# Scores of a head pair in one step over four PSUM banks, spatial mixing over 128 rows, and a new order of work

## The chip, the cores and the metric

The kernel runs on one core of one Trainium2 chip. The metric is device microseconds of one execution, lower is better; the median of three runs before the change is 319.94 us (319.62 to 322.25). Engines are named as in the profile: PE is TensorE's matmuls and PEld its weight loads, DVE is VectorE, ACT is ScalarE, POOL is GpSimd, SP is SyncE, whose queue issues the transfers.

## The reference

Three layers follow each other. All matrices are fp32, batch 2, sequence 448, model width 768.

```python
# 1: causal attention, 12 heads of 64
scores = where(causal, -1e9, q @ k.T / 8);  scores -= scores.max(-1)
a = exp(scores);  a = a / (a.sum(-1) + 1e-9);  x = a @ v
# 2: gated mixing along the sequence
h = gelu_tanh(x @ w_in);  u, v = h[..., :512], h[..., 512:]
v = (v - mean) / sqrt(var + 1e-6) * g_ln
v = einsum('ts,bsd->btd', w_sg, v) + b_sg          # the "spatial" mixing
x = x + (u * v) @ w_out
# 3: four attention experts, the best two of x @ w_gate by softmax weight
for e in range(4):
    out += weight[e] * (softmax(causal(q_e @ k_e.T / 8)) @ v_e @ wo[e])
```

## The kernel before

Everything stays on chip between the layers. Layer 1 works on pairs of heads: q and k of a pair are loaded (`qk_load`), rearranged into a `pair` tile by one copy, transposed on PE and copied to `qt` and `kt` with one head on rows 0 to 63 and the other on rows 64 to 127 (`qk_pair`). Scores of a pair are matmuls with 64 contraction rows, one head in each half of the PE array, side by side. The 448 query rows are four blocks (one of 64 rows and three of 128), causal, so that a head's scores fill two PSUM banks: bank 0 holds blocks 1 and 2 (192 and 320 keys), bank 1 holds block 3 (448 keys) and the 64-row block 0 (64 keys). `scores1(p, bank)` is one planner step for one bank of both heads. Then, for each head and bank, `bank_chain` runs: DVE adds the mask and takes the row maximum while it empties the bank (`tm`, L407), ACT takes the exponential and its sum (L414), DVE adds 1e-9 to the sums (L419) and takes reciprocals (L421), POOL or DVE scales `p` (L428, L430; in layer 3 with the gate, L426), PE transposes `p` (L434), and a copy brings it to `pt` (L359 on ACT, L361 on DVE). `pair_chain` multiplies by v (L460): 128 rows, 64 output columns a head, seven groups of matmuls for each head. Layer 3 does the same for two pairs of experts in each batch (`scores3`, L1148).

An fp32 matmul shows as two PE instructions (two passes); PE transposes and the float32r matmuls, which the projections use with high and low halves of each operand (three products each; L720, L681, L1181), show as one.

Layer 2 has the first projection in two parts: u in the transposed layout (`u_chain`, L720), v in the plain one (`v_chain`), both with a gelu. `sg_chain` transposes w_sg on PE (L825): four pieces of 112 rows and a fifth, a copy of the first 64 columns, because block 0 of both batches lies in one tile, batch 0 on rows 0 to 63 and batch 1 on rows 64 to 127. `spatial` (L909) is four fp32 matmuls in one PSUM bank: three over 128 rows and one over the 64 rows of block 0. Weights of w_in and w_out come as 64-bit words and are made into fp32 by ACT and DVE (`split64`, L504 to L510), then split into halves.

The order of all engines is set by a planner in the kernel (`Order`). Each piece of work is a generator that yields steps with a cost for each engine that may run them, buffers that they take (rings) and marks that they need. The planner keeps a clock for each engine and emits the step that can start first, within a slack by rank; ranks, biases for engines, buffer counts and the cost formulas are the numbers in `R`, `BIAS`, `SIZE` and the cost functions. What it emits is fixed at build time: on the chip each engine runs its list in order. The transfers are nearly all on SP's queue.

Of the kernel before, what the change touches and what calls it, by code (L numbers as in the profile page):

```python
# [58 lines left out]
def mm(n):  # L59
    return 2 + n / 2.4  # L60
# [18 lines left out]
class Step:  # L79
# [3 lines left out]
    def __init__(self, cost, take=(), need=(), dma=0, issue=450, kind=None, rows=1.0):  # L83
        self.cost, self.take, self.need, self.dma, self.issue = cost, take, need, dma, issue
        self.rows = rows
        self.bias = BIAS.get(kind, {})


def op(take=(), need=(), kind=None, rows=1.0, **cost):
    return Step(cost, take, need, kind=kind, rows=rows)  # L90
# [10 lines left out]
class Order:  # L101
# [12 lines left out]
    BIAS = dict(T=0, A=300, V=800, G=-400, S=0, Z=0)  # L114
    LATE = dict(T=0, A=300, V=700, G=-300, S=0, Z=0)
    TURN = 190000

    def __init__(self):
        self.clock = dict.fromkeys("TAVGSZ", 600.0)
        self.chains = []  # L120
        self.marks = {}
        self.rings = defaultdict(list)
        self.held = Counter()
        self.hw = self.queue = 0.0
        self.t, self.e = 0.0, "Z"
        self.used = defaultdict(float)
        self.state = (0, False)

    WINDOW = 10240 / 3

# [52 lines left out]
    def begin(self, ch):  # L185
# [13 lines left out]
        for e, c in st.cost.items():  # L199
# [9 lines left out]
            if e == "T" and not self.warm(t):  # L209
                c *= 2  # L210
# [6 lines left out]
    SLACK = 60  # L217

    def run(self):
        slack = self.SLACK  # L220
        while self.chains:
            first = {}
            cands = defaultdict(list)
            for ch in self.chains:
                b = self.begin(ch)
                if b is not None:
                    cands[b[0]].append((b[1], ch[0], ch, b[2], b[3]))
# [8 lines left out]
            e, (t, _, ch, items, end) = best  # L236
# [12 lines left out]
            else:  # L249
                self.t, self.e = end, e  # L250
                if e == "T":
                    self.use(t, end, st.rows)
                if e != "Z":
# [5 lines left out]
BIAS = {'ev': {'G': 100},  # L259
 'r': {'G': -600},  # L260
 'vh': {'A': -400, 'G': -200, 'V': 300},
 'vl': {'A': 400, 'V': 100},
 'wh': {'G': 400},
 'wl': {'A': 100},
 'y': {'G': 200, 'V': -200}}
R = dict(
    PV=(556.5, 563), PV0=556, vp=(569.5, 557.4), gt=(557.3, 543.0), QK=(555.5, 558.9, 562, 564),
    S=(552.4, 557, 560.3, 563), WO=(665.7, 669.3), WO0=669, v=(511, 517), v0=509, sp=(526, 538.7),
    wo2=(556.3, 546), wout=519, w3=(533, 555, 544.7), wo3=594, load=-37, trans=-7, vgroup=10, vhead=10, y=4,
    wu=4, wustep=4, wuahead=2, wv=58, wvafter=17, u=34, ub=(498.7, 481), sgl=63, sgafter=19, sgt=507,  # L270
    caps=(4, 2, 3, 5, 8, 7), av=0.5, bank=0.125, halves=28, bank3=1.125, av3=3.0, y3=14,
)
# [10 lines left out]
def attention_moe_kernel(  # L283
# [97 lines left out]
    class Core:  # L381


        def __init__(self, stack, side, n, np32, npt):
# [7 lines left out]
            ring("sm" + n, [ct([P, 4], F32, f"sm{n}{i}", pool) for i in range(4)])  # L392
            for _, _, t in o.rings["sm" + n]:
                G.memset(t, 1.0)
            ring("bias" + n, [ct([P, 4], F32, f"bias{n}{i}", pool) for i in range(6)])

    def bank_chain(c, key, bank, s, pts, pt_of, gate=None, need=()):
# [15 lines left out]
        for n, (i, rs, cs) in enumerate(parts):  # L413
            A.activation(p32[rs, cs], tm[rs, cs], AF.Exp, bias=bias[rs, i : i + 1], scale=-1.0,  # L414
                         accum_out=sm[rs, n : n + 1])
        give("tm" + c.n, tm)
        give("bias" + c.n, bias)
        yield op(V=73)
        V.tensor_scalar(sm[:, 0:2], sm[:, 0:2], 1e-9, None, op0=ALU.add)  # L419
        yield op(V=90)  # L420
        V.reciprocal(sm[:, 0:2], sm[:, 0:2])  # L421
        e, = yield op(kind="pr", G=950, V=500, need=need)
        for n, (i, rs, cs) in enumerate(parts):
            x, r = p32[rs, cs], sm[rs, n : n + 1]
# [19 lines left out]
    def pair_chain(c, b, keys, pts, vv, need, yh, yl, mark, after):  # L444


        _, y = yield op(T=2150, take=(BY,), need=[*[("p", k, bank) for k in keys for bank in range(2)], *need])
# [43 lines left out]
    def split64(src, shape, hi, lo, mark, rank=None):  # L491
# [4 lines left out]
        e, raw = yield dma(n * 2.84, ("raw",))  # L496
# [71 lines left out]
    def qk_load(p):  # L568
        b, hp = divmod(p, NP)
        raws = []  # L570
        for n, src in (("qraw", q), ("kraw", k)):
            e, t = yield dma(637, (n,), [("load", p - 1)] if p else ())
# [5 lines left out]
        done(("load", p))  # L578
# [38 lines left out]
    def qk_used(p):  # L617
        left["q", p] += 1
        if left["q", p] == 2:
            give("qt", qk[p][0])  # L620
            give("kt", qk[p][1])

    pts1 = defaultdict(dict)

    def scores1(p, bank):
# [12 lines left out]
        qk_used(p)  # L638
        for j, s in enumerate(ss):
            h = 2 * p + j  # L640
            o.add(2 * h + bank * R["bank"] * 8, bank_chain(core1, h, bank, s, pts1[h], lambda h=h: pt1_of(h)))
# [121 lines left out]
    for p in range(NPAIR):  # L763
        o.add(4 * p + R["load"], qk_load(p))
        for bank in range(2):
            o.add(4 * p + bank, scores1(p, bank))
# [16 lines left out]
    wsg, wvh, wvl = [], [], []  # L783
# [4 lines left out]
    def open_c2():  # L788
# [11 lines left out]
        for c in range(4):  # L800
            wsg.append(ct([P, SG], F32, f"wsg{c}", c2))
        u2[1] = [ct([P, S], F32, f"u2_1_{f}", c2) for f in range(4)]
# [486 lines left out]
```

## Time and profile before

| | before |
|---|---|
| timed runs, median (range) | 319.94 us (319.62 to 322.25) |
| profiled execution: span from first to last instruction | 317.5 us |
| busy in the span: PE | 302.2 us (95%) |
| DVE | 191.4 us (60%) |
| ACT | 173.7 us (55%) |
| POOL | 184.8 us (58%) |
| last chain: PE, POOL, DVE | 52%, 23%, 11% |

The profiled execution has no time of its own beside its span; the median of the timed runs is 2.44 us more than the span. PE instructions overlap in the records, so a share of 95% does not say that PE does useful work all the time. How closely matmuls follow each other is read from their start times.

Layer 1 lasts until the last L460 group, which starts at 125.34 us; the last `L1181` matmul is followed by one copy and the last transfer out.

### The profile page before, as it was taken

What the parts mean: (1) busy time and instruction counts of PE and PEld (TensorE: products, weight loads), DVE (VectorE), ACT (ScalarE), POOL (GpSimd) and SP (SyncE); (2) the same over time, 40 slices, a digit from 0 to 9 for tenths busy, and PEclk for the clock granted to TensorE, in tenths of its full rate; (3) what the DMA queues carried; (4) which work ended last, traced back from release to release, by engine and by line L of the source; (5) the groups of instructions that cost most, each with busy time, mean ns of one, the idle gap of its engine ahead of it and who ended that gap; (6) DMA issues with size and microseconds to landing.
All of it is one profiled execution on the core that took longest, in us unless ns stands there. A gap on an engine that the chain in (4) does not pass through costs nothing.

```text
span 317.5 us, 5926 instructions
## 1 busy us (share of the span) xinstructions
PE 302.2 (95%) x1928; PEld 231.7 (73%) x1928; DVE 191.4 (60%) x648; ACT 173.7 (55%) x480; POOL 184.8 (58%) x307
## 2 busy tenths in 40 slices
PE   6489999999999998999999999999999999999994
PEld 5256766677667785987886434999988977797794
DVE  4848797965887898535989512489714344175200
ACT  2748989877998886344646300222106148346742
POOL 3487589863854676542768899899981045004400
PEclk9969999999999999999999999999999999999999
DMA  7997372415600242225432200043100000000134
GB/s 198 223 217 209 110 182 85 125 62 124 200 1 3 59 134 78 64 39 165 130 99 53 49 0 0 2 99 77 49 24 9 12 0 2 0 2 2 52 118 180
DMA packets 38287, 25.70 MB, mean 81 GB/s; under 512 B 25904, under 2 KB 35696, under 8 KB 38256
## 3 DMA queue, kind: packets, MB, share of 16 engines
q1 hardware_dynamic: 38256, 25.32, 29.8%
q8 instruction: 15, 0.25, 0.3%
q14 instruction: 16, 0.13, 0.1%
HBM read 22.43 MB, written 2.75 MB: 79 GB/s over the span
## 4 chain that ended last, share of the span: by engine, by line
PE 52%; POOL 23%; DVE 11%; issue 5%; DMA 3%; ACT 3%; SPq 1%; POOLq 0%; DVEq 0%; ACTq 0%
PE bank L681 14%; PE bank L460 9%; PE bank L434 8%; PE bank L636 6%; PE bank L720 6%; PE bank L1181 5%; POOL xl L366 4%; POOL p L430 4%; POOL gl L366 3%; POOL big L915 3%; PE bank L1148 3%; POOL big L933 2%; DMA kraw<-in_k_dram 2%; DVE tm L407 2%; DVE w L508 2%
## 5 line engine op out<-in xcount | busy, mean ns | idle before, releaser
L430 POOL TENSOR_SCALAR p<-p,sm 128x192 f32<-128x192 f32 (+1 forms) x94 | 49.6, 540 | 29.0 <-DVE sm L419 9.0
L414 ACT ACTIVATE p<-tm,bias 128x320 f32<-128x320 f32 (+3 forms) x128 | 63.9, 505 | 3.5 <-DVE bias L407 3.4
L434 PE MATMUL bank<-ident,p 128*128 128x128 f32 x256 | 40.5, 286 | 4.6 <-POOL p L430 4.2
L359 ACT COPY pt<-bank 128x512 f32<-128x512 f32 x58 | 33.0, 585 | 15.6 <-PE bank L434 14.8
L426 POOL TENSOR_SCALAR p<-p,sm,gates 128x448 f32<-128x448 f32 (+3 forms) x28 | 15.6, 567 | 42.7 <-DVE gates L1054 30.7
L407 DVE CUSTOM_DVE_ANT_0 tm<-bank,maskw 128x448 f32<-128x448 f32 (+2 forms) x96 | 39.6, 436 | 0.0
L434 PEld LDWEIGHTS bank<-ident,p 128*128 128x128 f32 x256 | 28.5, 143 | 14.7 <-POOL p L430 9.6
L636 PE MATMUL bank<-kt,qt 64*128 64x192 f32 (+3 forms) x192 | 29.7, 419 | 2.0 <-ACT kt L359 2.0
L460 PE MATMUL bank<-pt,v_raw 128*64 128x128 f32 (+3 forms) x336 | 27.5, 314 | 0.1
L419 DVE TENSOR_SCALAR sm<-sm 128x2 f32<-128x2 f32 x64 | 16.5, 258 | 17.8 <-ACT p L414 16.7
L909 PE MATMUL bank<-wsg,vn 128*128 128x448 f32 (+1 forms) x64 | 27.1, 563 | 0.0
L460 PEld LDWEIGHTS bank<-pt,v_raw 128*64 128x64 f32 x336 | 20.1, 137 | 8.5 <-issue 3.8
L636 PEld LDWEIGHTS bank<-kt,qt 64*128 64x128 f32 (+1 forms) x192 | 14.1, 177 | 14.9 <-issue 10.1
L414 ACT ACTIVATION_READ_ACCUMULATOR p<-tm,bias 128x1 f32 (+1 forms) x128 | 24.7, 193 | 0.0
L909 PEld LDWEIGHTS bank<-wsg,vn 128*128 128x128 f32 (+1 forms) x64 | 10.9, 188 | 15.8 <-issue 15.7
L407 DVE CUSTOM_DVE_ANT_0 tm<-bank,mask 128x192 f32<-128x192 f32 x32 | 11.2, 349 | 16.3 <-PE bank L1148 13.1
L504 ACT ACTIVATE w<-raw 128x384 f32<-128x384 f32 (+1 forms) x22 | 12.9, 590 | 11.3 <-DMA raw<-in_moe_w_in_dram 6.9
L508 DVE SCALAR_TENSOR_TENSOR w<-raw,w 128x384 int32<-128x384 int32 (+1 forms) x22 | 18.6, 853 | 0.3
L720 PE MATMUL bank<-xh,wuh 128*128 128x448 f32 x48 | 18.6, 388 | 0.0
L720 PE MATMUL bank<-xl,wuh 128*128 128x448 f32 x48 | 18.0, 375 | 0.0
L720 PE MATMUL bank<-xh,wul 128*128 128x448 f32 x48 | 17.8, 378 | 0.0
L681 PE MATMUL bank<-gh,wuh 128*128 128x448 f32 x48 | 17.6, 367 | 0.0
(173 smaller groups left out, 746.3 us busy)
## 6 DMA issues: line engine op xcount, KB each, us to landing
raw<-in_moe_w_in_dram SPq DMA_DIRECT2D x8, 384.0 KB, 5.2
raw<-in_moe_w_in_dram SPq DMA_DIRECT2D x6, 512.0 KB, 5.5
raw<-in_moe_w_out_dram SPq DMA_DIRECT2D x8, 384.0 KB, 3.2
qraw<-in_q_dram SPq DMA_DIRECT2D x12, 224.0 KB, 3.3
kraw<-in_k_dram SPq DMA_DIRECT2D x12, 224.0 KB, 3.3
v_raw<-in_v_dram SPq DMA_DIRECT2D x18, 128.0 KB, 4.1
out_dram<-ot SPq DMA_DIRECT2D x3, 384.0 KB, 2.3
raw<-in_moe_w_sg_dram SPq DMA_DIRECT2D x2, 392.0 KB, 3.6
```

The lines of the kernel that those rows point to most:

```text
L359: A.copy(dst, src)
L366: (V if e == "V" else G).tensor_sub(dst, a, b_)
L407: V.tensor_tensor_reduce(out=tm[rs, cs], in0=s[rs, cs], in1=masks[i][rs], scale=-0.125, scalar=3.0e38, op0=ALU.add, op1=ALU.min, accum_out ...
L414: A.activation(p32[rs, cs], tm[rs, cs], AF.Exp, bias=bias[rs, i : i + 1], scale=-1.0, accum_out=sm[rs, n : n + 1])
L430: G.tensor_scalar(x, x, r, 0.0, op0=ALU.mult, op1=ALU.add)
L434: T.transpose(t[:, to * P : to * P + P], p32[:, blk * P : blk * P + P], ident)
L460: T.matmul(out_, lhsT=x[:, j, :], rhs=rhs, start=(n == 0), stop=(n == len(FLIPS) - 1), skip_group_check=True)
L508: V.scalar_tensor_tensor(t, low, 29, t, op0=ALU.logical_shift_right, op1=ALU.bitwise_or)
L636: T.matmul(s[:m, c0 : c0 + n], lhsT=qt[rows, QCOL[i] : QCOL[i] + m], rhs=kt[rows, k0 : k0 + n], start=True, stop=True)
L681: T.matmul(o_, lhsT=a, rhs=b_, start=(i == 0), stop=(i == n - 1))
L720: T.matmul(t[:, :S], lhsT=ks[0][a], rhs=ks[1][b_], start=(c == 0 and i == 0), stop=(c == NC - 1 and i == 2))
L909: T.matmul(t[:, :S], lhsT=vn[b][i][rows, fs], rhs=wsg[i][rows, ts_], start=(j == 0), stop=(j == 3))
```

## The change

Five things are done.

1. `scores1` and `scores3` are one step for a pair: all four banks (two of each head) are taken at once, and the sixteen fp32 passes follow each other. Block 0 loads 128 weight columns instead of 64 and writes 128 output rows (the lower 64 are not used; layer 3's `q3` tiles get 64 zero columns behind them).
2. `spatial`'s fourth matmul runs over 128 rows: block 0's weights are kept once with zeros on rows 64 to 127 (`wsg[0]`) and once with zeros on rows 0 to 63 (`wsg0`). The fifth piece of `sg_chain` goes; each of its copies is now two or three smaller ones on ACT.
3. q and k of the next pairs no longer wait for the pair before in `qk_load`, and rings have new sizes (`qraw` 4, `kraw` 3, `raw` 6, `p32` 5, `w32` 1, `big` 2, `pair` 2). On SP, q and k of the second pair stand ahead of w_in.
4. The sums tile has a 1e-9 beside each sum, written once; a DVE reduction over the two replaces the addition of 1e-9.
5. The planner has new costs (among them a price for a matmul of another array shape: `mode`, `TURNS`), biases and ranks, and so another order and another choice of engines.

```diff
+    TURNS = (150, 205, 205)
-            if e == "T" and not self.warm(t):
-                c *= 2
+            if e == "T":
+                if not self.warm(t):
+                    c *= 2
+                if st.mode != self.mode:
+                    c += self.TURNS[st.mode]
-    BIAS = dict(T=0, A=300, V=800, G=-400, S=0, Z=0)
+    BIAS = dict(T=450, A=-100, V=800, G=350, S=0, Z=0)
...
             ring("sm" + n, [ct([P, 6], F32, f"sm{n}{i}", pool) for i in range(4)])
             for _, _, t in o.rings["sm" + n]:
                 G.memset(t, 1.0)
+                G.memset(t[:, 1:4:2], 1e-9)
...
-        V.tensor_scalar(sm[:, 0:2], sm[:, 0:2], 1e-9, None, op0=ALU.add)
+        V.tensor_reduce(sm[:, 4:6], sm[:, 0:4].rearrange("p (n e) -> p n e", e=2), axis=AX.X, op=ALU.add)
         yield op(V=90)
-        V.reciprocal(sm[:, 0:2], sm[:, 0:2])
+        V.reciprocal(sm[:, 4:6], sm[:, 4:6])
...
-            e, t = yield dma(637, (n,), [("load", p - 1)] if p else ())
+            e, t = yield dma(800, (n,))
...
-        _, *ss = yield op(T=(950, 1000)[bank], take=(BS, BS))
-        for i in BANKS[bank]:
-            _, c0, n = PLACE[i]
-            m = 64 if i == 0 else P
-            k0 = KEYS[i][0]
-            for s, rows in zip(ss, (TOP, LOW)):
-                T.matmul(s[:m, c0 : c0 + n], lhsT=qt[rows, QCOL[i] : QCOL[i] + m],
-                         rhs=kt[rows, k0 : k0 + n], start=True, stop=True)
+        _, *ss4 = yield op(T=1800, mode=1, take=(BS, BS, BS, BS))
+        for bank in range(2):
+            ss = ss4[2 * bank : 2 * bank + 2]
+            for i in BANKS[bank]:
+                _, c0, n = PLACE[i]
+                k0 = KEYS[i][0]
+                for s, rows in zip(ss, (TOP, LOW)):
+                    T.matmul(s[:, c0 : c0 + n], lhsT=qt[rows, QCOL[i] : QCOL[i] + P],
+                             rhs=kt[rows, k0 : k0 + n], start=True, stop=True)
...
+        yield op(G=450)
+        G.memset(wsg[0][LOW], 0.0)
+        yield op(G=450)
+        G.memset(wsg0[0][TOP], 0.0)
...
-        for c, n in ((0, CP), (1, CP), (2, CP), (3, CP), (0, 64)):
-            c0 = S if n == 64 else c * CP
-            T.transpose(t[:, c0 : c0 + n], sg_raw[c // 2][1][:n, c % 2, sc * P : sc * P + P], ident[:n, :n])
+        for c in range(4):
+            T.transpose(t[:, c * CP : c * CP + CP], sg_raw[c // 2][1][:, c % 2, sc * P : sc * P + P], ident[:CP, :CP])
...
-            i, rows = (j + 1, slice(0, P)) if j < 3 else (0, HALF[b])
-            T.matmul(t[:, :S], lhsT=vn[b][i][rows, fs], rhs=wsg[i][rows, ts_], start=(j == 0), stop=(j == 3))
+            i = (j + 1) % 4
+            w = wsg0[0] if b and i == 0 else wsg[i]
+            T.matmul(t[:, :S], lhsT=vn[b][i][:, fs], rhs=w[:, ts_], start=(j == 0), stop=(j == 3))
```

Counted over all PE instructions of the two built programs, the shape of the array changes from one matmul to the next 126 times before and 56 times now. Scores stood in 29 uninterrupted groups (32 bank steps) and stand in 15 (16 pair steps).

The list of SP at its start, before (`qraw` and `kraw` are the landing tiles of a pair's q and k, with buffer numbers; `raw` those of weights):

```order
L573 DMA qraw_183<-in_q_dram 112x2x256
L573 DMA kraw_185<-in_k_dram 112x2x256
L497 DMA raw_102<-in_moe_w_in_dram 128x3x256
L497 DMA raw_103<-in_moe_w_in_dram 128x3x256
L497 DMA raw_104<-in_moe_w_in_dram 128x3x256
L556 DMA v_raw_180<-in_v_dram 64x4x64
L558 DMA v_raw_180<-in_v_dram 64x4x64
L573 DMA qraw_184<-in_q_dram 112x2x256
L573 DMA kraw_186<-in_k_dram 112x2x256
```

The same list with the change:

```order
L589 DMA qraw_191<-in_q_dram 112x2x256
L589 DMA kraw_195<-in_k_dram 112x2x256
L589 DMA qraw_192<-in_q_dram 112x2x256
L589 DMA kraw_196<-in_k_dram 112x2x256
L513 DMA raw_102<-in_moe_w_in_dram 128x3x256
L513 DMA raw_103<-in_moe_w_in_dram 128x3x256
L513 DMA raw_104<-in_moe_w_in_dram 128x3x256
```

The second pair's two transfers have moved from eighth and ninth to third and fourth place, ahead of three w_in transfers, and the first v transfers stand behind the loads of later pairs.

PE's list in layer 1 before, at the second pair (scores are `bank<-kt,qt`, transposes of `p` are `bank<-ident,p`, those of q and k `bank<-ident,pair`):

```order
L636 MATMUL bank_93<-kt_193,qt_191 128x192
L636 MATMUL bank_95<-kt_193,qt_191 128x192
L636 MATMUL bank_93<-kt_193,qt_191 128x320
L636 MATMUL bank_95<-kt_193,qt_191 128x320
L434 MATMUL bank_96<-ident,p_154 128x128 x4
L589 MATMUL bank_97<-ident,pair_188 128x112 x4
L636 MATMUL bank_98<-kt_193,qt_191 128x448
L636 MATMUL bank_92<-kt_193,qt_191 128x448
L636 MATMUL bank_98<-kt_193,qt_191 64x64
L636 MATMUL bank_92<-kt_193,qt_191 64x64
L434 MATMUL bank_91<-ident,p_155 128x128 x4
```

PE's list with the change, at the third pair:

```order
L450 MATMUL bank_91<-ident,p_153 128x128 x4
L648 MATMUL bank_93<-kt_204,qt_200 128x192
L648 MATMUL bank_94<-kt_204,qt_200 128x192
L648 MATMUL bank_93<-kt_204,qt_200 128x320
L648 MATMUL bank_94<-kt_204,qt_200 128x320
L648 MATMUL bank_95<-kt_204,qt_200 128x448
L648 MATMUL bank_96<-kt_204,qt_200 128x448
L648 MATMUL bank_95<-kt_204,qt_200 128x64
L648 MATMUL bank_96<-kt_204,qt_200 128x64
```

The two banks of a pair stand together, and the 64-column matmuls write 128 rows. Transposes no longer stand between them.

DVE's list with the change, at the start of layer 1 (`sm` are the sums, `tm` the masked scores; `ISA` is the mask and maximum with its read-out):

```order
L435 TENSOR_REDUCE sm_167<-sm_167 128x2
L435 TENSOR_REDUCE sm_168<-sm_168 128x2
L437 RECIPROCAL sm_167<-sm_167 128x2
L437 RECIPROCAL sm_168<-sm_168 128x2
L444 TENSOR_SCALAR p_153<-p_153,sm_167 128x192
L444 TENSOR_SCALAR p_153<-p_153,sm_167 128x320
L435 TENSOR_REDUCE sm_169<-sm_169 128x2
L423 ISA tm_151,bias_183<-bank_95,maskw 128x448
L423 ISA bias_183 128x1
```

Scalings of `p` now stand on DVE between the reductions and the masks of the next bank. In layer 1, 30 of the 48 banks' scalings are on DVE (1 before) and 18 on POOL; in the whole program POOL has 159 rows instead of 312, DVE 764 instead of 647 and ACT 409 instead of 354. Of layer 1's copies to `kt`, `qt` and `pt`, eleven move from DVE to ACT, and four more `pair` copies are on ACT.

## Rows read from the trace of the kernel before

**Rows 1.** Windows: busy time of each engine (and instructions), PEclk, DMA share, GB/s.
```profile
0.00:24.50 24.50, 15.77 (x92) 11.47 (x92) 13.72 (x57) 12.28 (x36) 13.29 (x33) 0.86 0.90 207
...
24.50:127.60 103.10, 100.75 (x835) 72.26 (x835) 83.81 (x326) 87.79 (x264) 68.70 (x121) 1.00 0.38 106
...
14.30:21.10 6.80, 4.43 (x19) 2.94 (x19) 3.56 (x17) 3.34 (x12) 6.16 (x8) 0.50 1.11 237
...
313.50:317.50 4.00, 0.02 (x1) 0.00 (x0) 0.00 (x0) 0.48 (x1) 0.00 (x0) 1.00 0.35 127
```
**Rows 2.** Timeline of the start: start us, us, engine, line, tiles, shape, count, idle before.
```profile
5.78 0.46 SPq L573 DMA_DIRECT2D kraw<-in_k_dram  x1
...
12.84 0.43 DVE L361 COPY pair<-kraw 112x512 f32<-112x512 f32 x1 [1.21 <-DMA kraw<-in_k_dram]
...
13.32 0.99 PE L589 MATMUL bank<-ident,pair 112*128 112x112 f32 x8 [2.97 <-DVE pair L361]
...
17.98 2.08 PE L636 MATMUL bank<-kt,qt 64*128 64x192 f32 x8
...
21.50 1.28 PE L636 MATMUL bank<-kt,qt 64*128 64x448 f32 x8
```
**Rows 3.** Waits of PE: who waited for whom, us in total, times, longest.
```profile
PE bank L434 <- POOL p L430: 4.2, 7, 1.9
```
**Rows 4.** Timeline of PE in layer 1, the two banks of scores apart.
```profile
94.37 1.13 PE L636 MATMUL bank<-kt,qt 64*128 64x192 f32 x8
95.44 1.09 PE L434 MATMUL bank<-ident,p 128*128 128x128 f32 x8
...
99.69 0.66 PE L434 MATMUL bank<-ident,p 128*128 128x128 f32 x4
100.27 1.28 PE L636 MATMUL bank<-kt,qt 64*128 64x448 f32 x8
101.49 1.09 PE L434 MATMUL bank<-ident,p 128*128 128x128 f32 x8
...
101.65 0.49 PE L434 MATMUL bank<-ident,p 128*128 128x128 f32 x3
```
**Rows 5.** Timeline of PE in layer 3, both banks together, and its later passes.
```profile
239.34 2.15 PE L1148 MATMUL bank<-k,q 64*128 64x192 f32 x16
...
240.68 0.54 PE L1148 MATMUL bank<-k,q 64*128 64x448 f32 x2
...
241.16 0.27 PE L1148 MATMUL bank<-k,q 64*64 64x64 f32 x2
...
241.42 0.39 PE L681 MATMUL bank<-wvh,xl 128*128 128x260 f32 x1
```
**Rows 6.** Timeline of PE in the spatial mixing: four passes of one chain.
```profile
175.03 0.54 PE L909 MATMUL bank<-wsg,vn 128*128 128x448 f32 x1
...
175.78 0.54 PE L909 MATMUL bank<-wsg,vn 128*128 128x448 f32 x1
...
177.68 0.54 PE L909 MATMUL bank<-wsg,vn 128*128 128x448 f32 x1
```
**Rows 7.** Single lines: operation and count, duration ns min/median/max, first and last start.
```profile
L419 DVE TENSOR_SCALAR sm<-sm x64: 135/169/1259, 13.2 to 296.9; 128x2 f32<-128x2 f32 x64
...
L1012 DVE TENSOR_REDUCE m<-lg x2: 169/170/171, 250.0 to 281.8; 128x4 f32<-128x16 f32 x2
...
L361 DVE COPY kt<-bank x5: 269/594/625, 62.6 to 94.5; 128x448 f32<-128x448 f32 x4, 128x128 f32<-128x128 f32 x1
```
**Rows 8.** Groups by line and shape: count | busy us, mean ns | idle before.
```profile
L359 ACT COPY kt<-bank 128x448 f32<-128x448 f32 x8 | 4.2, 526 | 1.6 <-PE bank L589 1.5
...
L419 DVE TENSOR_SCALAR sm<-sm 128x2 f32<-128x2 f32 x64 | 16.5, 258 | 17.8 <-ACT p L414 16.7 <-POOL p L430 0.8
...
L428 DVE TENSOR_SCALAR p<-p,sm 128x448 f32<-128x448 f32 x1 | 1.4, 1378 | 0.1
...
L426 DVE TENSOR_SCALAR p<-p,sm,gates 128x320 f32<-128x320 f32 x2 | 1.0, 498 | 0.0
```

More of the change, by code (lines that the diff above doesn't have):

```diff
@@ L235, in run @@
                     best = (e, x)
-            e, (t, _, ch, items, end) = best
+            e, (_, _, ch, items, end, t) = best
             st = ch[4]
@@ L444, in pair_chain @@
     def pair_chain(c, b, keys, pts, vv, need, yh, yl, mark, after):
-        _, y = yield op(T=2150, take=(BY,), need=[*[("p", k, bank) for k in keys for bank in range(2)], *need])
+        _, y = yield op(T=2060, mode=2, take=(BY,), need=[*[("p", k, bank) for k in keys for bank in range(2)], *need])
         for n, (j, at, num, step, i) in enumerate(FLIPS):
@@ L764, in attention_moe_kernel @@
         o.add(4 * p + R["load"], qk_load(p))
-        for bank in range(2):
-            o.add(4 * p + bank, scores1(p, bank))
+        o.add(4 * p, scores1(p))
         o.add(4 * p + R["av"], pair1(p))
@@ L829, in sg_chain @@
                 give("raw", sg_raw[i][0])
-        e, = yield Step(copies_ps(SG))
-        copy(e, wsg[sc], t)
+        rs = slice(0, P) if sc else TOP
+        for x, rows, to, fr, n in ((wsg[sc], rs, 0, 0, S), (wsg[sc], rs, S, 0, 64), *(() if sc else ((wsg0[0], LOW, 0, 0, S),))):
+            e, = yield Step(copies_ps(n))
+            copy(e, x[rows, to : to + n], t[rows, fr : fr + n])
         give(BC, t)
@@ L1130, in pair3, with scores3 @@
                               [("lg", b, j) for j in range(4)], lambda: yh, lambda: yl, ("y3", b, pe), lambda: None)
[L1132 to L1138 removed]
+    def scores3(b, pe, rank):
         yield wait(("wq", "p", b, pe), ("wk", "p", b, pe))
         qt, kt = qk3["wq", b, pe], qk3["wk", b, pe]
[L1142 to L1155 removed]
+        _, *ss4 = yield op(T=1800, mode=1, take=(BS, BS, BS, BS))
+        end = o.t
+        for bank in range(2):
+            ss = ss4[2 * bank : 2 * bank + 2]
+            o.t = end - 950 * (1 - bank)
+            for i in BANKS[bank]:
+                _, c0, n = PLACE[i]
+                k0 = KEYS[i][0]
+                for s, rows in zip(ss, (TOP, LOW)):
+                    T.matmul(s[:, c0 : c0 + n], lhsT=qt[rows, BLOCKS[b][i] : BLOCKS[b][i] + P],
+                             rhs=kt[rows, k0 : k0 + n], start=True, stop=True)
+            for i, s in enumerate(ss):
+                e = 2 * pe + i
+                o.add(rank + i + bank * R['bank3'],
+                      bank_chain(st["core"], (b, e), bank, s, pts3[b, e], lambda e=e: pt3_of((b, e)),
+                                 st["gates"][b][:, :, e : e + 1], [("gates", b)]))
+        o.t = end
+        give("q3", qt)
+        give("k3", kt)
     def open_ot():
@@ L1242, in attention_moe_kernel @@
                 o.add(R['QK'][2 * b + pe], proj_qk(b, pe, n))
-            for bank in range(2):
-                o.add(R['S'][2 * b + pe] + bank, scores3(b, pe, bank, R['S'][2 * b + pe]))
+            o.add(R['S'][2 * b + pe], scores3(b, pe, R['S'][2 * b + pe]))
             o.add(R['S'][2 * b + pe] + 1 + R['av3'], pair3(b, pe))
```

126 lines of the change are left out of this document (58 added, 68 removed).

## The prediction

> **What bounds the kernel now.** I read the windows first, because the page's shares are averages. From 24.5 to 127.6 us PE is busy 100.75 of 103.10 us; in the first 24.5 us only 15.77, partly at a granted clock of 0.50 (1.2 GHz, from 14.3 to 21.1 us); after its last matmul 4.0 us remain for a copy and the last transfer [rows 1]. In the view of waits the largest of PE is 4.2 us for the scalings on POOL [rows 3]. So PE's queue is the bound nearly everywhere after the start, and the question is what its time consists of. Busy time cannot tell, since records overlap. Start times can.
>
> Look at a group of transposes between two groups of scores. In the group from 101.49 us the first takes 0.16 us to the next start (101.49 to 101.65); from there to its last start (101.49 + 1.09, less a record of 0.27, is 102.31) six steps take 0.11 each. But four transposes ahead of scores take 0.58 (99.69 to 100.27), where 0.44 would do [rows 4]. The missing 0.15 are about 0.05 at the first and 0.09 at the last: PE pays where the array's shape (128 rows by 128 columns, 64 by 128, 64 by 64, 128 by 64) changes. That price, times the changes of shape counted in the order, is my sum. The other engines come second: in layer 1 ACT and DVE are busy 87.79 and 83.81 of 103.10 us [rows 1], and whatever shortens PE there takes idle time from them.
>
> **The change part by part.**
>
> *Scores as one step.* Apart, the banks take 1.07 (94.37 to 95.44) and 1.22 us (100.27 to 101.49), 2.29 together [rows 4]. Where they happen to stand together they take 2.08 (239.34 to 241.42) [rows 5]. That is 0.21 in the scores' own records, and 0.15 in the transposes on both sides: 0.36 for each group that disappears. 29 groups become 15: 14 x 0.36 = 5.0 us, nearly all in layer 1.
>
> *The 64-row block with 128 columns.* The last 448-column pass before the 64-column form takes 0.48 (240.68 to 241.16), where one takes 0.375 [rows 5, 6]; the change of shape, 0.10, goes in each of 16 steps: 1.6 us. The passes behind it (0.26 with the exit, 241.16 to 241.42) must now load 128 weight columns each. No row has so few moving columns with so many weights; the nearest is the 128-column transpose at 0.11 [rows 4]. If a pass is faster than I think, up to 0.05 more a step is gained (0.8); if two loads for the two halves follow one another, 0.11 a step is lost (1.7). I take no difference, since one pass of 0.11 and one with its exit come near the 0.26.
>
> *Mixing over 128 rows.* Two passes over 128 rows take 0.75 (175.03 to 175.78). The last of them, two over 64 rows and the first behind take 1.90 (175.78 to 177.68) where four would take 1.50 [rows 6]: 0.40 a chain, 8 chains, 3.2 us. Streaming zeros costs nothing extra, as a pass lasts as long with 64 rows. The two memsets on POOL run while PE still does first projections.
>
> *The fifth piece of the w_sg transposes.* Four pieces go, each a change of shape in and out. By the transposes' prices, 0.05 and 0.09 on the neighbours and 0.11 or more of its own, 0.25 each: 1.0 us. The five extra copies on ACT stand in a stretch where seven v groups still lie between them and their reader.
>
> Together 10.8 us of PE's queue, bounds 9.0 (loads following one another) to 11.7.
>
> *q and k of the second pair ahead of w_in.* Before, the second k is issued at 5.78 and lands at 12.84; DVE waits 1.21 for it in its list with the sums of pair 0 behind, and PE idles 2.97 us [rows 2]. Then both score groups of that pair run at 17.98 (2.08 us, at the low clock) and 21.50 (1.28). Now they are the third and fourth transfers, and the whole step follows the first pair's. The first transposes of `p` come no earlier for that: ahead of them DVE masks several banks. So the gain is the 3.36 us of work which move into idle time, less 0.4 for two more warm-up matmuls: 3 us. Bounds: 0, if DVE delays everything behind by as much, and 5, if less of the first 24.5 us is at the low clock too. What w_in loses is covered: its first reader on PE stands far behind the third pair.
>
> *1e-9 and the choice of engines.* The additions on DVE have a median of 169 ns, but a mean of 258 and a maximum of 1259; reductions of about that size take 170, every one [rows 7, 8]. 64 x 0.09 = 5.6 us come off DVE, 4.2 of it in layer 1. The Trainium skill, SBUF — State Buffer, "Who interferes with whom", gives a rule for both: DVE and GpSimd share a port pair under an exclusive lock; tensor_scalar can take it, tensor_reduce never does. The spread of 135 to 1259 agrees. By the rule the reductions stay flat and DVE gains the whole 5.6, but the new scalings can block, as in rival B; if reductions spread as the additions do, DVE gains nothing. My sum for PE is the same by both.
>
> ACT gets eleven copies from DVE and four `pair` copies: 15 x 0.53 = 7.9 us [rows 8], all in layer 1. Its cover is its idle time: 103.1 - 87.8 = 15.3 us after 24.5 us [rows 1]. Layer 1 is to become shorter by 4.3 (12 of the 14 groups) and 1.2 (12 steps), so 15.3 - 5.5 - 7.9 = 1.9 us would be left: not enough for nobody to wait. Against it stands that POOL's slow scalings, for which PE waited 4.2 us [rows 3], are fewer. I take 3 us of new stalls in layer 1; bounds 0 (the planner's order keeps PE fed) and 9 (ACT at its share of before plus some, rival A).
>
> Sum against the profiled execution: 317.5 - 10.8 - 3 + 3 = 306.7 us of span. The median of the timed runs is 2.44 above the span, and I leave that: **309.1 us**. In layers 2 and 3 I expect no new stalls: PE's chains are as long as before, and POOL's slow subtractions have gone to DVE.
>
> **The rivals.**
>
> A: *ACT becomes the bound of layer 1.* If its share after 24.5 us can't rise above the 0.85 of before (87.79 / 103.10), it needs (87.79 + 7.9) / 0.85 = 112.6 us, 9.5 more than before; forecast were 103.1 - 5.5 + 3 = 100.6, so 12.0 are lost: 321.1 us, no change. For it: ACT's list is in order, and each exponential waits for DVE. Against it: at 0.85 it was not the bound but waited for PE's transposes, and PE itself runs at 0.98. At a share of 0.91 it would be 105.2 us, and 313.7.
>
> B: *DVE's scalings block, and DVE becomes the bound: slower.* The one ungated scaling of 448 on DVE took 1378 ns [rows 8]. At that price, 30 banks in layer 1 add 41 us to DVE's 83.81 + 13.72 = 97.5; eleven copies (0.59 each [rows 7]) and 4.2 for the sums go, 10.7. That is 128 us of work, which starts some 4 us into the span; with 5% idle it ends at 139, 17 us behind the 122.1 that I expect for the end of layer 1 (127.6 - 5.5 - 3 + 3): 326 us. It decides from about 0.85 us a bank on (86.8 + 30 x 0.85 = 112, 95% of the 118 us to be had), and the kernel is slower by over 1% from about 1.3. Against it: gated ones of 320 took 498 [rows 8], which with 192 columns more makes some 0.8 a bank, just short of it; and POOL, the other party, has 18 of its 47 scalings left in layer 1.
>
> C: *the start and layer 1 both go well*: 11.7 off PE, 5 at the start, no stalls: 317.5 - 16.7 + 2.44 = 303.2.
>
> **How the numbers follow.** My forecast with its bounds (from 303 up to 317.5 - 9.0 - 0 + 6 + 2.44 = 316.9) gets 0.70: the changes of shape are counted, and their prices repeat to 0.01 us in the groups that I compared. C gets 0.08, A 0.14, B 0.08. A range from 303 to 317 holds the forecast, C's edge and the milder half of A. About 1%, 3.2 us, is what a measurement of this kernel can tell. Below 316.7 lie the forecast, C and a third of A: 0.82. Within 1% lie the rest of A and the mildest of B: 0.11. B otherwise: 0.07.
>
> **What would show it.** In the changed kernel's timeline a score step should take 2.0 us, 0.07 to 0.1 less than the 2.08 of both banks together, and transposes before and behind it what they do now. A chain of the mixing should take 3.0 us (8 x 0.375) instead of 3.4. The last group of the values' matmuls (125.34 us before) should start near 119 to 120. If it starts after 125, rival A or B holds: then ACT's or DVE's busy share after the start is near 1, or PE waits for `tm`, `p` or `pt` in the view of waits. The DVE rows of the scalings decide on B: a mean of bank 1's 448 near 0.5 us clears it, over 1 us makes it. The forecast is wrong in its main term if PE's start-to-start times at a change of shape differ from those of before, or if the time after layer 1 does not shrink by about 4 us.

## The result, and the profile of the changed kernel

The changed kernel takes 303.35 us (median of four runs, 302.91 to 304.8) where the kernel before takes 319.96 in the same measurement. The ratio is 0.948 (95% interval 0.943 to 0.953). Measured again among the runs told of below, it took 303.34 us, ratio 0.949 (0.945 to 0.952). One of the five executions of the kernel with 64 weight columns below took 364.25 us at a granted clock of 0.755 and is left out of its numbers. That is 16.6 us less, where 10.8 were forecast. The time lies only 0.35 us inside the lower end of the range, where rival C stood, so the 5.8 us that were missed need as much of an explanation as direction and main mechanism.

The windows of the changed kernel (columns as in [rows 1]):

```profile
0.00:24.50 24.50, 19.87 (x142) 16.18 (x144) 16.61 (x78) 18.16 (x53) 8.88 (x35) 1.00 0.90 222
24.50:118.60 94.10, 93.06 (x809) 72.95 (x805) 85.06 (x353) 87.43 (x265) 30.84 (x51) 1.00 0.45 116
118.60:297.00 178.40, 178.13 (x984) 147.81 (x982) 119.72 (x338) 90.86 (x219) 36.42 (x69) 1.00 0.17 47
```

In the first 24.5 us PE has 142 instructions where it had 92. Behind that its share is 0.99, ACT's is 87.43 / 94.10 = 0.93 (0.85 before) and DVE's 0.90 (0.81 before). PE's largest waits in this execution:

```profile
PE bank L450 <- DVE p L444: 2.9, 4, 1.9
PE bank L772 <- DVE b_half L338: 1.1, 1, 1.1
PE bank L450 <- POOL p L446: 1.0, 1, 1.0
```

The 4.2 us for POOL of [rows 3] have become 1.0, and the waits for `pair` and `kt` are gone. PE's timeline at the start, a merged score step, and the last matmuls with the values:

```profile
1.05 5.06 PE L772 MATMUL bank<-b_half 128*128 128x128 f32 x22 [1.05 <-DVE b_half L338]
5.90 1.45 PE L604 MATMUL bank<-ident,pair 112*128 112x112 f32 x8
...
8.41 3.89 PE L648 MATMUL bank<-kt,qt 64*128 64x192 f32 x32
14.16 1.47 PE L450 MATMUL bank<-ident,p 128*128 128x128 f32 x8 [1.86 <-DVE p L444]
...
20.85 2.05 PE L648 MATMUL bank<-kt,qt 64*128 64x192 f32 x16
22.83 2.29 PE L476 MATMUL bank<-pt,v_raw 128*64 128x384 f32 x28
...
112.59 2.29 PE L476 MATMUL bank<-pt,v_raw 128*64 128x384 f32 x28
```

A score step takes 22.83 - 20.85 = 1.98 us. The groups of 28 that follow (L476) are the landmarks of this section: twelve of them stand in layer 1. In the kernel before the first and the last are:

```profile
26.53 2.29 PE L460 MATMUL bank<-pt,v_raw 128*64 128x384 f32 x28
...
125.34 2.29 PE L460 MATMUL bank<-pt,v_raw 128*64 128x384 f32 x28
```

In the changed kernel the last group starts at 112.59, well ahead of the 119 to 120 us that the prediction names. First and last group cut both executions into three parts. Two corrections make the parts comparable. Ahead of its first group the changed kernel has done eight more transposes of `p` and eight more score passes, and four fewer q/k transposes: 8 x 0.109 + 1.05 - 4 x 0.095 = 1.5 us. Behind its last group it still has 64 matmuls of the u projection to do, the kernel before 54: 10 x 0.20 = 2.0 us. PE's last matmul ends at 297.09 and 313.52.

| part | before | after | difference | corrected | forecast |
|---|---|---|---|---|---|
| to the first group | 26.53 | 22.83 | -3.7 | -5.2 | -4.0 |
| first to last group | 98.81 | 89.76 | -9.05 | -5.5 | -1.5 |
| from the last group to PE's end | 188.18 | 184.50 | -3.7 | -5.7 | -5.3 |

The prediction gives its terms for layer 1 as a whole; the column divides them by where the work stands. Of layer 1's twelve score steps three stand ahead of the first group of values (the line at 8.41 is two of them) and nine behind it, and of the twelve groups of scores that disappear there, two and ten. So the forecast of the first part is the start (-3) with 2 x 0.36 + 3 x 0.10 of changes of shape, and that of the middle part 10 x 0.36 + 9 x 0.10 = 4.5 us less and +3 of new stalls. Layer 3 and the mixing came out nearly as worked out; layer 1 behind its start gave 4.0 us more than was thought and the start 1.2.

In the last part the w_sg transposes can be read by themselves, before (a second such group runs from 144.25 to 145.67) and now:

```profile
138.59 1.49 PE L825 MATMUL bank<-ident,raw 112*128 112x112 f32 x10
140.01 0.50 PE L681 MATMUL bank<-wvnh,xh 128*128 128x512 f32 x1
```

```profile
117.09 1.70 PE L842 MATMUL bank<-ident,raw 112*128 112x112 f32 x16
118.56 0.45 PE L734 MATMUL bank<-xh,wuh 128*128 128x448 f32 x1
```

They took 1.42 us twice and take 1.47 once: 1.4 us less, where 1.0 was forecast.

Rows of the costs in dispute, by line and shape (count | busy us, mean ns | idle before):

```profile
L435 DVE TENSOR_REDUCE sm<-sm 128x2 f32<-128x4 f32 x64 | 9.1, 146 | 4.3 <-ACT p L430 4.0
...
L444 DVE TENSOR_SCALAR p<-p,sm 128x448 f32<-128x448 f32 x13 | 7.3, 565 | 0.4
L444 DVE TENSOR_SCALAR p<-p,sm 128x320 f32<-128x320 f32 x17 | 6.5, 382 | 0.0
...
L444 DVE TENSOR_SCALAR p<-p,sm 128x192 f32<-128x192 f32 x17 | 6.1, 357 | 0.6
...
L444 DVE TENSOR_SCALAR p<-p,sm 64x64 f32<-64x64 f32 x13 | 3.8, 293 | 0.0
```

A bank's scalings on DVE cost 0.357 + 0.382 = 0.74 us or 0.565 + 0.293 = 0.86 us, at rival B's point of decision (0.85) but far from the 1.3 from which the kernel would be slower.

### The profile page after: what moved, and what is told of

It reads as the page before. It is cut to its first block, busy times and chain, and to the rows that moved or that the text cites. A ratio compares the mean times of both kernels' runs of the same rounds, so it can differ in the third digit from the quotient of the medians.

```text
span 301.0 us, 5882 instructions
## 1 busy us (share of the span) xinstructions
PE 291.2 (97%) x1928; PEld 236.9 (79%) x1928; DVE 221.4 (74%) x765; ACT 196.9 (65%) x535; POOL 76.1 (25%) x154
## 4 chain that ended last, share of the span: by engine, by line
PE 67%; DVE 14%; ACT 7%; issue 3%; POOL 1%; DMA 1%; POOLq 0%; ACTq 0%; DVEq 0%
PE bank L695 33%; PE bank L929 8%; PE bank L734 7%; PE bank L476 5%; DVE tm L423 5%; PE bank L450 5%; PE bank L1202 4%; ACT p L430 3%; PE bank L648 2%; PE bank L1167 2%; DVE p L444 2%; ACT pt L374 2%; DVE p L442 1%; DVE sm L437 1%; DMA kraw<-in_k_dram 1%
## 5 line engine op out<-in xcount | busy, mean ns | idle before, releaser
L430 ACT ACTIVATE p<-tm,bias 128x192 f32<-128x192 f32 (+3 forms) x128 | 64.0, 506 | 5.8 <-DVE bias L423 5.3
L374 ACT COPY pt<-bank 128x512 f32<-128x512 f32 x58 | 32.6, 589 | 11.0 <-PE bank L450 10.8
L446 POOL TENSOR_SCALAR p<-p,sm 128x448 f32<-128x448 f32 (+3 forms) x36 | 19.5, 552 | 52.2 <-DVE sm L437 28.7
L476 PE MATMUL bank<-pt,v_raw 128*64 128x128 f32 (+3 forms) x336 | 27.4, 314 | 0.0
L476 PEld LDWEIGHTS bank<-pt,v_raw 128*64 128x64 f32 x336 | 19.7, 137 | 8.3 <-issue 4.5
L648 PE MATMUL bank<-kt,qt 64*128 64x192 f32 (+3 forms) x192 | 24.4, 395 | 0.1
L929 PE MATMUL bank<-wsg,vn 128*128 128x448 f32 x64 | 24.2, 539 | 0.0
L648 PEld LDWEIGHTS bank<-kt,qt 64*128 64x128 f32 x192 | 16.7, 186 | 8.3 <-issue 5.4
L444 DVE TENSOR_SCALAR p<-p,sm 128x192 f32<-128x192 f32 (+3 forms) x60 | 21.2, 395 | 1.0
L929 PEld LDWEIGHTS bank<-wsg,vn 128*128 128x128 f32 x64 | 12.2, 190 | 11.6 <-issue 11.1
L381 POOL TENSOR_TENSOR wul<-w,wuh 128x384 fp32r<-128x384 f32 x12 | 12.5, 1041 | 26.5 <-ACT wuh L374 26.3
L695 PE MATMUL bank<-gl,wuh 128*128 128x448 f32 x48 | 17.5, 365 | 0.0
L695 PE MATMUL bank<-gh,wul 128*128 128x448 f32 x48 | 17.4, 365 | 0.0
```

The source lines that it names most:

```text
L374: A.copy(dst, src)
L381: (V if e == "V" else G).tensor_sub(dst, a, b_)
L444: V.tensor_scalar(x, x, r, None, op0=ALU.mult)
L446: G.tensor_scalar(x, x, r, 0.0, op0=ALU.mult, op1=ALU.add)
L476: T.matmul(out_, lhsT=x[:, j, :], rhs=rhs, start=(n == 0), stop=(n == len(FLIPS) - 1), skip_group_check=True)
L648: T.matmul(s[:, c0 : c0 + n], lhsT=qt[rows, QCOL[i] : QCOL[i] + P], rhs=kt[rows, k0 : k0 + n], start=True, stop=True)
```

## The experiments

All start from the changed kernel, and all but the last version of the start leave the order of other work as it is, so that one thing changes at a time. Diffs are shortened, and comments in them are added here. The twelve runs were made in three groups on three chips, each beside the kernel before (319.55, 319.93 and 319.47 us). The changed kernel stood in the second, so a difference across groups is good to about half a microsecond at best.

> The changed kernel itself, unaltered, as the base for the runs beside it: 302.9 to 304.8 us, with a granted clock between 0.988 and 1.0 from one execution to the next, as in its first runs.

It took 303.34 us (303.16 to 303.58). From the first to the last group of values its trace has 89.81 us, 0.05 from the first profile, although the granted clock from 14.3 to 24.5 us was 0.83 in the one and 1.00 in the other. That stretch serves as a ruler below (89.8 us).

### Are the changes of shape what the merged step saves?

```diff
         for bank in range(2):
+            if bank == 1:
+                T.transpose(ss[0][:, :P], ident, ident)
             for i in BANKS[bank]:
```

> The changed kernel with one dummy 128 by 128 transpose (of the identity, into the bank that the next pass overwrites) between the two banks of each of the 16 score steps: the array's shape changes twice more a step, no other order changes. Theory (the turn is what the merged step saves): the transposed block itself 0.11 us and the two turns 0.36, so 16 x 0.47 = 7.5 us above the changed kernel: 303.4 + 7.5 = 310.9 us. Rival (back-to-back matmuls of any shape cost their columns, and the gain came from elsewhere): 16 x 0.11 = 1.8 us, 305.2, the same as with the dummy among the transposes.

For the control the same transpose stands among the transposes of `p`:

```diff
             T.transpose(t[:, to * P : to * P + P], p32[:, blk * P : blk * P + P], ident)
+            if blk == 0 and bank == 0 and even:
+                nxt = SLOTS[bank][1]
+                T.transpose(t[:, nxt * P : nxt * P + P], ident, ident)
```

> The control for the kernel with dummies between the banks: the same 16 dummy transposes, but each stands behind the first transpose of p of one bank per pair, where the shape is the same before and behind. Theory and rival agree: 16 x 0.10 = 1.6 us above the changed kernel, 305.0 us. The difference of the two is the price of the turns alone: 5.8 us by the theory, 0 by the rival.

Measured: 307.9 us (ratio 0.964, 0.962 to 0.967) and 304.04 us (0.952, 0.949 to 0.955). The difference is 3.9 us, where the theory said 5.8 and the rival 0. The control itself is 0.7 us above the changed kernel, where 1.6 to 1.8 us of dummies were put in. PE's timeline with the dummy between the banks (L645):

```profile
30.13 1.13 PE L650 MATMUL bank<-kt,qt 64*128 64x192 f32 x8
31.19 0.33 PE L645 MATMUL bank<-ident 128*128 128x128 f32 x1
31.45 1.19 PE L650 MATMUL bank<-kt,qt 64*128 64x448 f32 x8
32.57 1.09 PE L450 MATMUL bank<-ident,p 128*128 128x128 f32 x8
```

The step takes 32.57 - 30.13 = 2.44 us, 0.46 more than 1.98: 0.10 for the transpose and 0.36 for the turns, the price of the prediction to 0.01 us. But it doesn't all reach the end. From the first to the last group of values the trace has 117.54 - 25.41 = 92.13 us with dummies between the banks:

```profile
25.41 2.29 PE L476 MATMUL bank<-pt,v_raw 128*64 128x384 f32 x28
...
117.54 2.29 PE L476 MATMUL bank<-pt,v_raw 128*64 128x384 f32 x28
```

and 113.26 - 23.06 = 90.20 in the control:

```profile
23.06 2.29 PE L480 MATMUL bank<-pt,v_raw 128*64 128x384 f32 x28
...
113.26 2.29 PE L480 MATMUL bank<-pt,v_raw 128*64 128x384 f32 x28
```

That is 1.9 more. In this stretch stand nine dummies between the banks, and eleven in the control:

```profile
L645 PE MATMUL bank<-ident 128*128 128x128 f32 x9 | 3.0, 328 | 0.0
```

```profile
L454 PE MATMUL bank<-ident 128*128 128x128 f32 x11 | 3.0, 272 | 0.0
```

So 9 x 0.46 - 11 x 0.11 = 2.9 us more were put in, and two thirds of it arrive. Behind layer 1 the two differ by 1.7, with 4 x 0.36 = 1.4 put in. So the price is shown, and so is that layer 1 passes on about two thirds of it. The rest stood there already as waits. They are short and show on PE's weight loads (PEld) of the transposes of `p`; between 26 and 119 us in the control, then with the dummies between the banks:

```profile
PEld bank L451 <- DVE p L445: 1.4, 4, 0.6
PEld bank L451 <- POOL p L447: 1.1, 4, 0.3
```

```profile
PEld bank L450 <- DVE p L444: 0.7, 3, 0.4
PEld bank L450 <- POOL p L446: 0.7, 2, 0.5
```

A slower PE waits 1.1 us less for `p` here, about the microsecond that doesn't arrive.

### Block 0 with 128 weight columns, and the mixing over 128 rows

```diff
-    T.matmul(s[:, c0 : c0 + n], lhsT=qt[rows, QCOL[i] : QCOL[i] + P],
+    m = 64 if i == 0 else P                      # in layer 3 too
+    T.matmul(s[:m, c0 : c0 + n], lhsT=qt[rows, QCOL[i] : QCOL[i] + m],
```

> The changed kernel with block 0's scores loaded with 64 weight columns again (64 output rows), in the merged step. Theory (the last pass ahead pays 0.10 us for the change from 64 by 128 to 64 by 64, the passes themselves last the same): 16 x 0.10 = 1.6 us slower, 305.0 us. Rival 1 (loading 128 columns for 64 moving ones costs as much as the turn): no change, 303.4. Rival 2 (the 128 loads overlap better): 2.4 us slower, 305.8.

It took 304.0 to 305.7 us, ratio 0.953 (0.950 to 0.956), some 1 us above the changed kernel. That is the sign of the theory, and less than its 1.6; the interval of about 0.9 us either way doesn't separate it from no change.

```diff
-    T.matmul(t[:, :S], lhsT=vn[b][i][:, fs], rhs=w[:, ts_], ...)
+    r = HALF[b] if i == 0 else slice(0, P)
+    T.matmul(t[:, :S], lhsT=vn[b][i][r, fs], rhs=w[r, ts_], ...)
```

> The changed kernel with the mixing's fourth matmul over the 64 rows of block 0 again (the halves with zeros are not read). Theory: 0.40 us a chain for the change of shape, 8 chains, 3.2 us slower: 306.6 us, if PE is the bound of that stretch. Rival (PE waits for v groups or DVE there anyway): under 1 us slower, with PE's waits shorter by the rest.

Measured: 306.13 us, ratio 0.957 (0.955 to 0.959), 2.8 more. The line of the mixing in the changed kernel, then with 64 rows (duration min/median/max, first and last start):

```profile
L929 PE MATMUL bank<-wsg,vn x64: 539/539/539, 158.4 to 182.1; 128*128 128x448 f32 x64
```

```profile
L930 PE MATMUL bank<-wsg,vn x64: 536/539/644, 158.5 to 185.1; 128*128 128x448 f32 x48, 64*128 64x448 f32 x16
```

The 64 passes stretch from 23.7 to 26.6 us from first to last start. With every row used, one follows another each 23.7 / 63 = 0.376 us, a chain of eight in 3.0. The view of waits shows none of PE in this stretch, and nearly all of the 3.2 arrives. No transposes stand between these passes, so the price, 2.9 us for eight chains or 0.36 a chain, belongs to the change of shape and not to transposes as such.

### What the second pair's q and k are worth

```diff
-            queue(e).dma_start(out=..., in_=src[b, 2 * hp : 2 * hp + 2]...)
+            f_ = lambda: queue(e).dma_start(out=..., in_=src[b, 2 * hp : 2 * hp + 2]...)
+            late.append(f_) if p == 1 else f_()      # issued behind the third w_in transfer
```

> The changed kernel with q and k of the second pair issued behind the three w_in transfers instead of ahead of them; every engine's list but SP's start is the same. Theory (the place of these two transfers is what the start gained): DVE and PE wait for them in order, the second pair's scores start some 4 us later, and the kernel takes 3 to 4.5 us more, 306.4 to 307.9 us, with the granted clock at 0.98 to 0.99 as in the kernel before. Rival (layer 1 has slack enough behind the start to take it up): under 1 us more, 304.

Measured: 309.91 us, ratio 0.969 (0.966 to 0.972), 6.6 us more, twice the forecast's term and above this expectation. Its timeline and its waits:

```profile
11.91 1.94 PE L611 MATMUL bank<-ident,pair 112*128 112x112 f32 x8 [4.93 <-DVE pair L376]
13.78 4.93 PE L655 MATMUL bank<-kt,qt 64*128 64x192 f32 x32
...
29.58 2.29 PE L478 MATMUL bank<-pt,v_raw 128*64 128x384 f32 x28
```

PE waits 4.9 us for the second pair, and then the score steps of both pairs take 4.93 us where they took 3.89. All of the loss is there at the first group of values (29.58 against 22.83, 6.75); behind it the ruler shows 119.38 - 29.58 = 89.80 as ever. The window tells why the steps are slower:

```profile
8.20:14.30 6.10, 2.39 (x12) 1.84 (x14) 0.85 (x2) 0.95 (x2) 0.00 (x0) 0.57 1.13 247
```

After PE has stood still from 7 to 11.9 us, the mean granted clock of the stretch to 14.3 is 0.57, so much of it lies at the lower level of 1.2 GHz, as in the kernel before behind its 2.97 us of idle time [rows 1, 2]. To tell the clock from the wait, the next kernel computes dummies in that gap:

```diff
-        for _ in range(n):                       # behind the first pair: 1 dummy
+        for _ in range(n if n > 5 else 24):
```

> The kernel with q and k of the second pair behind w_in (309.9 us), with 24 dummy matmuls instead of one behind the first pair's transposes, so that PE computes instead of idling from 6.6 to about 11.9 us. It tells the wait apart from the clock. Theory (the late transfers cost 4.9 us of waiting, and the fall of the clock behind the idle time the rest): the granted clock stays at 1.0 from 8.2 to 14.3 us and the time falls by 1.5 to 2.5 us to 307.4 to 308.4. Rival (all of it is waiting): 309.9, at whatever clock.

Measured: 307.94 us, ratio 0.964 (0.961 to 0.967): 2.0 less by the medians, which are of two groups, and 1.5 less by the ratios. Its window and its timeline:

```profile
8.20:14.30 6.10, 6.10 (x55) 5.72 (x55) 0.85 (x2) 1.12 (x4) 0.00 (x0) 1.00 1.10 244
```

```profile
13.60 3.89 PE L655 MATMUL bank<-kt,qt 64*128 64x192 f32 x32
...
28.02 2.29 PE L478 MATMUL bank<-pt,v_raw 128*64 128x384 f32 x28
```

The two steps are back at 3.89 us, although the transfers are as late, and the first group of values comes 29.58 - 28.02 = 1.56 us earlier. So of the 6.6 us of the place in the queue, 1.5 to 2.0 were the clock and the rest, 4.6 to 5.1, the wait.

### The warm-ups, and a version meant to be faster

```diff
-        for _ in range(n):                       # 11 warm-ups
+        for _ in range(n if n < 5 else 7):
```

> The changed kernel with 7 warm-up matmuls emitted ahead of the first q and k transposes instead of 11 (their results are read by nobody). In the changed kernel's timeline the pair copies are done at about 4.8 us and PE's first transposes start only at 5.9, behind the warm-ups. Theory (the start is the chain of PE's warm-ups, transposes, scores, masks): everything behind them moves up by about 1.1 us: 302.2 us. Rival (the clock decides): the granted clock stays low longer or falls again, and the time is 1 to 3 us more, 304.4 to 306.4 us, with a mean granted clock under 0.99.

Measured: 303.87 us, ratio 0.951 (0.948 to 0.955): no difference that can be told, so the theory fell, and the rival with it, since four of the six executions kept a mean clock of 0.994 or more. PE's first transposes start at 4.24 instead of 5.90, but the second pair's k lands too late for the first scores to gain: its transposes wait 0.97 and the scores start at 8.48. So a last kernel takes the first pair's scores ahead of those transposes (and its first masks, exponentials and the second `kt`'s copies accordingly), with 7 warm-ups. In words:

```diff
 PE:  7 dummies; q, k of pair 0; dummy; q of pair 1
-     k of pair 1; scores of pair 0; scores of pair 1
+     scores of pair 0; k of pair 1; scores of pair 1
```

> A version that is to be faster than both: the changed kernel with 7 warm-ups instead of 11, and the first pair's scores on PE ahead of the second pair's k transposes (with their masks, exponentials, and the copies to the second kt in the matching place on DVE and ACT); all else in the same order. Theory (with 7 warm-ups alone the second pair's k, which lands at 7.4 us, is what the first scores wait behind): the first pair's scores start at about 7.0 us instead of 8.4, DVE's first mask at 8.3 instead of 9.7, and the time is 1 to 1.4 us less, 301.9 to 302.3. Rival (the start is bound elsewhere, by DVE's list or the clock, so that nothing moves): 303.3 us.

```profile
6.69 2.05 PE L333 MATMUL bank<-kt,qt 64*128 64x192 f32 x16
10.53 2.05 PE L332 MATMUL bank<-kt,qt 64*128 64x192 f32 x16 [1.25 <-ACT kt L333]
13.04 1.47 PE L332 MATMUL bank<-ident,p 128*128 128x128 f32 x8 [0.46 <-DVE p L332]
```

The first transposes of `p` start at 13.04 instead of 14.16, and its last group of values at 111.46 instead of 112.59. Yet the runs give 302.62 us (302.31 to 304.4), ratio 0.949 (0.945 to 0.952) like the changed kernel's: 0.7 us by the medians, too little to be told apart. The trace shows that the start moved by 1.1 us; that the kernel is faster is not shown.

### Why layer 1 didn't stall: POOL, ACT and the sums

```diff
         e, = yield op(kind="pr", G=950, V=500, need=need)
+        if gate is None:
+            e = "G"            # layer 1: all scalings on POOL
```

> The changed kernel with all scalings of p in layer 1 on POOL again, in the same place of the order (30 banks move from DVE). Theory (PE's waits in layer 1 came from POOL's slow scalings, and taking them away is why no stalls replaced them): PE's waits for p of POOL are above 4 us again and the time is 2 to 5 us more, 305.4 to 308.4. Rival (whoever scales, the order hides it, and DVE, relieved of some 23 us, runs ahead): no change or up to 1 us less, 302.4 to 303.4.

Measured: 308.52 us, ratio 0.965 (0.962 to 0.968), 5.2 more, just above the upper end of the theory. Its largest wait, and its first and last group of values:

```profile
PE bank L452 <- POOL p L448: 7.0, 11, 2.0
```

```profile
24.56 2.29 PE L478 MATMUL bank<-pt,v_raw 128*64 128x384 f32 x28
...
118.38 2.29 PE L478 MATMUL bank<-pt,v_raw 128*64 128x384 f32 x28
```

1.7 us are lost at the start, where the granted clock from 14.3 to 24.5 us was 0.67, and 93.82 - 89.8 = 4.0 in layer 1. POOL isn't full there (53.6 of 94.1 us busy); it is that a `p` stands behind others and copies in POOL's list while PE waits for it.

```diff
                          accum_out=sm[rs, 2 * n : 2 * n + 1])
+        if gate is None and bank == 1 and key % 2 == 0:
+            A.copy(spare, maskw)
```

> The changed kernel with one more ACT copy of 448 columns for each pair of layer 1 (a constant tile into a spare tile that nobody reads), behind the exponential of bank 1 of the pair's first head: 12 x 0.5 = 6 us more work for ACT, which is busy 87.4 of the 94.1 us behind the start. Theory of the prediction (ACT's idle time is the cover; when it is used up, PE stalls): 6.7 us were left, 0.7 remain, and with ACT's share held near 0.93 layer 1 takes some 6 us more: 307 to 309.4 us. Rival (ACT's idle time is not needed, since ACT's list runs ahead of its readers): under 1.5 us more, 303.3 to 304.8, with ACT's share of that stretch at 0.97 or more.

Measured: 305.7 us, ratio 0.957 (0.954 to 0.959), 2.4 more: between the two. The 12 copies were 6.7 us of work, ten of them (5.5 us) between the first and the last group of values. Window and groups:

```profile
24.50:118.60 94.10, 91.69 (x797) 71.58 (x794) 84.03 (x356) 89.89 (x273) 30.19 (x51) 1.00 0.42 115
```

```profile
23.96 2.29 PE L480 MATMUL bank<-pt,v_raw 128*64 128x384 f32 x28
...
115.75 2.29 PE L480 MATMUL bank<-pt,v_raw 128*64 128x384 f32 x28
```

ACT's share rises to 0.955, and the ruler to 91.79, 2.0 us more. So an added microsecond of ACT's work costs 2.0 / 5.5 = 0.36 there. Neither is ACT's idle time free, nor is it a wall.

```diff
-        V.tensor_reduce(sm[:, 4:6], sm[:, 0:4]..., axis=AX.X, op=ALU.add)
+        V.tensor_scalar(sm[:, 4:6], sm[:, 0:4:2], 1e-9, None, op0=ALU.add)
```

> The changed kernel with the addition of 1e-9 on DVE as before in place of the reduction over two, in the same place of the order. Theory (an addition can be held up by POOL's instructions, a reduction is not): the 64 additions take 0.2 to 0.26 us each with a maximum near 1 us, against 0.146 flat, DVE is busy 4 to 7 us more, and the time is 0.5 to 2 us more, 303.8 to 305.3 us. Rival (with most scalings on DVE, POOL is idle enough that additions take 0.13 to 0.15 us): no change, 303.3 us.

Measured: 305.35 us, ratio 0.956 (0.953 to 0.960), 2.0 more, the upper end of the theory. The additions there, against the reductions' 125/145/159 in the changed kernel:

```profile
L435 DVE TENSOR_SCALAR sm<-sm x64: 140/157/967, 12.9 to 282.1; 128x2 f32<-128x2 f32 x64
```

The medians are nearly the same; it is the tail that goes. All five additions over 230 ns began while an instruction on POOL was running and ended 19 to 27 ns behind its end; for the longest:

```profile
72.94 1.18 POOL L381 TENSOR_TENSOR wul<-w,wuh 128x384 fp32r<-128x384 f32 x1
73.18 0.97 DVE L435 TENSOR_SCALAR sm<-sm 128x2 f32<-128x2 f32 x1
```

Not every meeting does this: ten others overlapped POOL's work and took 228 ns or less. With a mean of 196 against 146 ns the additions cost 3.2 us more on DVE. The ruler shows 114.21 - 22.58 = 91.63, 1.8 us more. The rule that the prediction quoted (the Trainium skill, SBUF — State Buffer, "Who interferes with whom": tensor_scalar can be locked out by GpSimd, tensor_reduce can't) agrees with both maxima, 967 and 159 ns.

## Why the prediction was right, and where it was off

**The changes of shape (-10.8): right in price, two thirds passed on in layer 1.** The score step is 1.98 us (2.0 forecast), a mixing chain 3.0 (3.0), the turn of a separated bank 0.36 (0.36), and the passes of 64 columns with 128 weights cost the same 0.26 us as before, the value taken between the bounds. In the mixing and in layer 3 PE is the bound and the saving arrives whole: the last part fell by 5.7 against a forecast of 5.3 (the text's "about 4" was its own terms added up too low), and the w_sg piece, at 1.4 instead of 1.0, is the difference. In layer 1 only about two thirds arrive, since `p` is not always ready for a faster PE. The prediction had such a loss among its new stalls, but as ACT's doing; the waits seen are for `p` from DVE and POOL. The w_sg piece was read from the two timelines and not tried by itself.

**The start (-3): too small.** The table gives -5.2. Up to 1.0 of it are changes of shape, so 4.2 to 5.2 are left for the term, at the upper end of its bounds (0 to 5). The undoing gives 6.6, but with 4.93 us of idle PE where the kernel before had 2.97. The direction and the way were right: the scores of two pairs now fill the idle time. The work moved was priced, but the clock only as a bound: 1.5 to 2.0 us of the place in the queue are the clock that doesn't fall, since PE's gap is gone.

**New stalls in layer 1 (+3): the step that failed.** The middle part fell by 5.5, not 1.5. ACT's side of the term was about right: 15 copies, 7.9 us, at 0.36 are an estimated +2.8. (The upper end of the range was added up with +6, though the term's own bound was 9.) What was mis-sized is the other side: POOL's scalings were named as a counterweight and got no number, and the shorter sums were said to leave PE's sum alone. By the ruler the first is worth 4.0 us and the second 1.8. From these, an estimate for the middle part is -3.0 (4.5, two thirds passed on) - 4.0 - 1.8 + 2.8 = -6.0, against the -5.5 of the table. The undone parts do not add up exactly: turns (3.9 x 14 / 16 = 3.4), 1.0, 2.8, 6.6, 5.2 and 2.0 make 21.0 us, ACT's copies take 2.8 off, and 18.2 is 1.6 more than was measured, though the w_sg piece is not among them. Each part was undone in an order that was planned with it, which may be the reason; the planner's new order and the ring sizes were not undone by themselves, so what they give or cost stays open.

**The rivals.** A: ACT's share rose from 0.85 to 0.93 in layer 1, and 0.955 was reached, so 0.85 was no ceiling. B: the scalings on DVE take 0.74 and 0.86 us a bank; the blocked 1378 ns of [rows 8] is not seen, the longest of 60 is 845 ns. C gave the time that came, 303.2, in part by luck: its start is close, but not all of its 11.7 arrives, and its "no stalls" hides two things of opposite sign, the price of ACT's work and the larger relief from POOL's scalings and the blocked additions.

## What to carry to other kernels

Price a change of array shape by start-to-start times and then ask, stretch by stretch, what share of a saved microsecond arrives: here nearly all of it in the mixing and layer 3, about two thirds in layer 1, and 0.36 of an added one on ACT. Where PE waits for an engine's result, give the relief of that engine a term of its own, as large as the wait that it ends. A landmark on PE with the same work behind it splits a difference into parts, and a stretch that repeats to 0.05 us is a finer ruler than the timed runs.

## What the runs showed of the hardware

- One 128 by 128 transpose between two groups of 64-row matmuls costs 0.46 us, 0.36 of it turns, the same as the two banks apart had cost.
- Five microseconds of idle PE at the start were followed by a mean granted clock of 0.57 from 8.2 to 14.3 us; the same gap filled with matmuls on zeros kept it at 1.00 and saved 1.5 to 2.0 us.
- Reductions over two columns on DVE lie between 125 and 159 ns in all 64; additions of two columns, with POOL at work, between 140 and 967, and the five longest end 19 to 27 ns behind a POOL instruction that had begun before them.
